# Two counting steps and three fine steps in the searches for experts 3 to 6

## The chip, the cores and the metric

The kernel runs on one core of a Trainium2 chip. The metric is the device time of one execution in microseconds (us), from profiles and timings on the chip. The engines named here are TensorE (PE in the profile, PEld for its weight loads), VectorE (DVE), ScalarE (ACT), GpSimd (POOL) and SyncE (SP), whose queue issues most DMAs.

## The reference

An attention with a decaying state makes 3072 rows of 384. A mixture of eight experts assigns each row to one expert, greedily by falling logit, with at most 384 rows per expert; each expert is a two-layer network. A second network with squared ReLU follows on all rows.

```python
logits = x @ w_gate
order = np.argsort(-logits.flatten())
for idx in order:
    tok, e = (int(idx) // E, int(idx) % E)
    if assigned[tok] >= 0 or counts[e] >= cap:
        continue
    assigned[tok] = e
    counts[e] += 1
for e in range(E):
    mask = assigned == e
    h = np.maximum(x[mask] @ w1[e], 0.0)
    out[mask] = h @ w2[e]
h = np.maximum(out @ w_in, 0.0)
return h * h @ w_out
```

## The kernel before

After the attention (its last part is over at about 105 us of the span) the kernel finds the experts one after another: the expert that fills first, its 384 rows, then the next among the rows and experts that are left. "Expert p" is the p-th one found, p = 0 to 7. The work on expert p, `expert(p)` and then `mlp(p)`, is a dense row of large matmuls of 384 columns; every product is made of three matmuls, from high and low parts (XH and XL, wh and wl, ah and al, YH and YL). ScalarE makes the high parts, VectorE or GpSimd the low ones.

The search for expert p+1 runs beside the work on expert p. `tick()` stands after each block of nine large matmuls, 47 times per expert (16 in `expert`, 31 in `mlp`), and there advances the generator `phase(p+1)` by one `yield`. Matmuls of the search are thus sown among the large ones in the order in which the program issues them; the order on TensorE and SP is this written order, and on VectorE, ScalarE and GpSimd it is made by the scheduler of the framework.

One step of a search (L697 to L773) tests 64 thresholds. VectorE compares 3072 keys (128 partitions x 24) with all of them in three operations (L537, called at L705); TensorE counts by expert in twelve small matmuls (L715), folds two halves with two more (L756) and sums the saturated ones with a matmul against ones (L765); VectorE takes the maximum (L769) and the new lower bound (L772). Four such steps give a bracket [lo, hi) for the threshold at which the expert fills. The selection follows (L782 on): it counts the sure and the possible rows (L793, L794), scans them, makes two staircases E0 and E1 over 384 slots (L814, L816), and turns them into row numbers by six matmuls (L823, L824); GpSimd gathers the rows (L840).

For p of 2 and more the gathered rows are transposed in blocks: SP writes them to a scratch in DRAM (`xb`) and reads them back in another order into two tiles of a ring of five (`raw64`), and VectorE transposes 32x32 blocks into PSUM (L867, alternately `misc` and `conv`), from which XH and XL are made. The copy at L866 holds each transpose behind the newest al. As soon as an expert is known, SP loads its weights (five raw tiles), which ScalarE and GpSimd split into wh (L926) and wl (L927).

The search for p+1 begins with the first tick of expert p. It needs 21 ticks to the selection and 41 to the last block.

Of the kernel before, what the change touches and what calls it, by code (L numbers as in the profile page):

```python
# [40 lines left out]
E = 8  # L41
# [3 lines left out]
BLOCKS = 2  # L45
# [415 lines left out]
class Routing:  # L461
# [4 lines left out]
    def __init__(self, tc, pool, ident, L):  # L466
# [5 lines left out]
        self.lag = 3, 1  # L472
# [187 lines left out]

    def phase(self, p, st, xd, rows, half):
# [6 lines left out]
        sc = w([128, 24], "scal")  # L668
        rs = w([128, 2], "rs", BF)
        scn = w([128, 2, NT], "scn")  # L670
        if last:
            for _ in range(18):
                yield
# [4 lines left out]
        else:  # L678
            if p:
                sh = [128, NT, E]  # L680
                lm = w(sh, "lm", FT, 1)
                if p == 2:
                    V.tensor_copy(lm[0:1, 0, 0:1], self.made())
                V.tensor_tensor(lm, self.L, pen[:, None, :].to_broadcast(sh), op=OP.add)
                m, key, cx, oh = w([128, NT], "m"), w([128, NT], "key"), w([128, NT], "cx"), w(sh, "oh", BF)
                V.tensor_reduce(m, lm, axis=AX.X, op=OP.max)
                V.tensor_tensor(key, m, dead, op=OP.add)
                for f in self.pick(lm, m, cx, oh, w(sh, "eq", FT, 1)):
                    f()
                yield  # L690

                base, d = self.low[:, 0:1], self.range
            else:
                key, cx, oh = self.key0, self.cx0, self.oh0
                base, d = self.s0[:, 0:1], self.s0[:, 1:2]
            steps = range(0 if p else 1, 4)
            for t in steps:  # L697
                fin = t == steps[-1]
                cnt = self.misc()
                thr = cnt[:, 256:256 + KG] if p else w([128, KG], "thr")  # L700
                V.tensor_scalar(thr, self.k[:, 1:], d, base, op0=OP.mult, op1=OP.add)
                cuts = (0, 8, 16, 24) if p else (0, 9, 18, 24)
                cms = []

                def cmp():  # L705
                    a, b = cuts[len(cms)], cuts[len(cms) + 1]
                    cms.append(w([128, b - a, KG], "cm", BF, 3))
                    self.compare(V, cms[-1], key[:, a:b], thr)

                def cmm(g):  # L710
                    for j in range(cuts[g], cuts[g + 1], 2 if p else 1):
                        i = j - cuts[g]
                        if p:

                            PE.matmul(cnt[:, :2 * E], cms[g][:, i:i + 2].rearrange("p j k -> p (j k)"),  # L715
# [599 lines left out]
```

## Time and profile before

| | before |
|---|---|
| median of 3 runs (lowest, highest) | 783.78 us (783.5, 786.86) |
| profiled execution: time | 782.99 us |
| its span, first to last instruction | 781.3 us |
| TensorE busy, matmuls | 757.0 us (97%) |
| VectorE busy | 432.2 us (55%) |
| ScalarE busy | 383.6 us (49%) |
| GpSimd busy | 300.3 us (38%) |
| mean granted TensorE clock, share of full speed | 0.983 |

"Busy" is the union of an engine's instructions over the span. Matmuls overlap in the pipeline, so that a busy TensorE is no proof that it works at its peak; distances from one start to the next are the better measure. An idle time is put down to the instruction that ended it. In a timeline the columns are start (us), duration (us), engine, line, operation, output and inputs, shapes and count; a count above one merges a row of equal instructions.

### The profile page before, as it was taken

The numbers are of one execution on the slowest core, as the hardware profiler recorded it, in microseconds if no ns is written. First come the engines' busy times: TensorE is split into PE (matmuls) and PEld (weight loads), VectorE is DVE, ScalarE is ACT, GpSimd is POOL, SyncE is SP. The second block draws the span as 40 slices with busy tenths as digits, with TensorE's granted clock in tenths as the row PEclk, the third lists the DMA queues.
The fourth block names the chain that finished last, engine by engine and source line by source line (L and its number), as shares of the span: only waits on it lengthen the run. The fifth ranks groups of instructions, "written<-read, shape, count | busy, mean of one in ns | idle before, by whom it ended". The sixth has DMA issues, their size and how long they took to land.

```text
span 781.3 us, 16728 instructions
## 1 busy us (share of the span) xinstructions
PE 757.0 (97%) x6388; PEld 713.1 (91%) x6389; DVE 432.2 (55%) x1118; ACT 383.6 (49%) x886; POOL 300.3 (38%) x321
## 2 busy tenths in 40 slices
PE   7999996899999999999999999999999999999996
PEld 4888874698999999999999999999999999999996
DVE  9899998988964554455445444534453423221210
ACT  3666651546662465346534643464346455452542
POOL 6899831667653061306130614060406072013001
PEclk9999995999999999999999999999999999999999
DMA  9988751674351071107010701070107040400000
GB/s 257 281 249 258 224 185 54 209 227 124 102 188 31 8 206 39 33 4 215 27 40 1 223 20 42 0 210 35 41 1 208 33 135 11 133 25 27 1 0 31
DMA packets 48689, 80.84 MB, mean 103 GB/s; under 512 B 14448, under 2 KB 36448, under 8 KB 48608
## 3 DMA queue, kind: packets, MB, share of 16 engines
q1 hardware_dynamic: 45536, 70.33, 30.3%
q0 software_dynamic: 3072, 9.44, 3.6%
q8 instruction: 50, 0.82, 0.5%
q14 instruction: 31, 0.25, 0.1%
HBM read 66.78 MB, written 12.98 MB: 102 GB/s over the span
## 4 chain that ended last, share of the span: by engine, by line
PE 86%; DVE 8%; DMA 2%; issue 2%; POOL 1%; ACT 1%; SPq 0%; POOLq 0%; DVEq 0%; ACTq 0%
PE acc L930 12%; PE ph L930 12%; PE acc L932 12%; PE acc L931 12%; PE ph L931 12%; PE ph L932 12%; PE pA L247 3%; PE pY L267 3%; DMA raw<-in_w_dram 2%; PE ph L1056 1%; PE pl L284 1%; PE pt L304 1%; PE pk L327 1%; PE pY L260 1%; PE misc L715 1%
## 5 line engine op out<-in xcount | busy, mean ns | idle before, releaser
L927 POOL TENSOR_TENSOR wl<-raw,wh 128x384 fp32r<-128x384 f32 x114 | 115.0, 1027 | 184.8 <-ACT wh L926 153.1
L1114 DVE TENSOR_TENSOR al<-ph,ah 128x384 fp32r<-128x384 f32 x105 | 58.4, 556 | 135.1 <-ACT ph L1106 134.8
L930 PE MATMUL ph<-YH,wi 128*128 128x384 f32 x384 | 132.1, 344 | 0.0
L931 PE MATMUL ph<-YL,wi 128*128 128x384 f32 x384 | 129.3, 337 | 1.2 <-DVE YL L1085 1.2
L930 PE MATMUL acc<-wo,ah 128*128 128x384 f32 x384 | 129.5, 337 | 0.0
L932 PE MATMUL acc<-wo,al 128*128 128x384 f32 x384 | 128.8, 335 | 0.7 <-POOL al L1114 0.7
L932 PE MATMUL ph<-YH,wi 128*128 128x384 f32 x384 | 128.9, 336 | 0.0
L931 PE MATMUL acc<-wo,ah 128*128 128x384 f32 x384 | 128.5, 335 | 0.0
L1099 ACT ACTIVATE t<-ph 128x384 f32<-128x384 f32 x128 | 62.1, 492 | 111.5 <-PE ph L932 100.3
L1132 POOL DMA_INDIRECT out_dram<-rows,idx x24 | 23.7, 988 | 205.0 <-ACT rows L1130 200.8
L926 ACT ACTIVATE wh<-raw 128x384 fp32r<-128x384 f32 x128 | 66.0, 523 | 74.2 <-DMA raw<-in_w_dram 24.6
L1066 DVE SCALAR_TENSOR_TENSOR al<-ph,ah 128x384 fp32r<-128x384 f32 x64 | 35.6, 556 | 82.8 <-ACT ah L1063 82.8
L931 PEld LDWEIGHTS ph<-YL,wi 128*128 128x128 f32 x384 | 72.2, 188 | 2.2 <-DVE YL L1085 2.0
L932 PEld LDWEIGHTS acc<-wo,al 128*128 128x128 f32 x384 | 72.1, 188 | 1.4 <-POOL al L1114 1.0
L930 PEld LDWEIGHTS ph<-YH,wi 128*128 128x128 f32 x384 | 72.2, 188 | 0.0
L930 PEld LDWEIGHTS acc<-wo,ah 128*128 128x128 f32 x384 | 72.1, 188 | 0.0
L931 PEld LDWEIGHTS acc<-wo,ah 128*128 128x128 f32 x384 | 72.1, 188 | 0.0
L932 PEld LDWEIGHTS ph<-YH,wi 128*128 128x128 f32 x384 | 72.1, 188 | 0.0
L1105 ACT ACTIVATE ah<-t 128x384 fp32r<-128x384 f32 x128 | 67.2, 526 | 2.7
L930 PE MATMUL acc<-ah,wh 128*128 128x384 f32 x192 | 66.3, 345 | 0.1
L932 PE MATMUL acc<-ah,wl 128*128 128x384 f32 x192 | 64.5, 336 | 0.6 <-POOL wl L927 0.6
L931 PE MATMUL acc<-al,wh 128*128 128x384 f32 x192 | 64.3, 335 | 0.0
(263 smaller groups left out, 1516.5 us busy)
## 6 DMA issues: line engine op xcount, KB each, us to landing
raw<-in_w_dram SPq DMA_DIRECT2D x128, 192.0 KB, 2.9
rk<-in_rk_dram SPq DMA_DIRECT2D x24, 448.0 KB, 5.3
tk<-in_tk_dram SPq DMA_DIRECT2D x24, 392.0 KB, 5.8
raw<-in_wi_dram SPq DMA_DIRECT2D x16, 384.0 KB, 3.6
raw<-in_wo_dram SPq DMA_DIRECT2D x16, 384.0 KB, 3.5
xd<-xs SPq DMA_DIRECT2D x24, 192.0 KB, 3.1
xb<-rows SPq DMA_DIRECT2D x18, 192.0 KB, 3.1
raw<-xb SPq DMA_DIRECT2D x18, 192.0 KB, 3.9
```

Of the source, the lines that this page charges most:

```text
L247: PE.matmul(pA[n][s][half(c, 64), i], RK[n][half(s), 1, i, 64 * c:64 * c + 64], RK[n][half(s), 0, i], start=True, stop=True)
L267: PE.matmul(pYs[n][s][half(i % 2, 64), i // 2], v_of(n, 2 * i + s), AM[n][:, i, s], start=not c and i < 2, stop=True, skip_group_check=True)
L926: A_.activation(hi, t, AF.Copy)
L927: (eng or G).tensor_tensor(lo, t, hi.bitcast(FT), op=OP.subtract)
L930: PE.matmul(o, l[0], r[0], start=first, stop=False)
L931: PE.matmul(o, l[0], r[1], start=False, stop=False)
L932: PE.matmul(o, l[1], r[0], start=False, stop=last)
L1066: V.scalar_tensor_tensor(hl, o, 0.0, hh.bitcast(FT), op0=OP.max, op1=OP.subtract)
L1099: A_.activation(t, o, AF.Relu)
L1105: A_.activation(gh, t, AF.Square)
L1114: (V if p else G).tensor_tensor(gl, t2, gh.bitcast(FT), op=OP.subtract)
L1132: h = G.indirect_dma_start(out=out, out_offset=bass.IndirectOffsetOnAxis(ap=st[p]["idx"][:, i:i + 1], axis=0), in_=t, in_offset=None)
```

## The change

For experts 3 to 6 a search has five steps. The first two are the counting steps of before, the second with a sixteenth as the next spacing. The three that follow test 16 thresholds by VectorE alone: the partition stands for one of 16 thresholds and one of 8 experts, and four operations compare 768 keys each and add up the result. For that the keys, masked by expert (`lay`, two operations), go to a scratch in DRAM (`kd`) in one DMA and come back in four, each to all 16 thresholds, in tiles of the ring `raw64`. A fine step has one matmul: the saturated flags, one column repeated as 128 columns of weights, against a constant `its`. That matmul stands five ticks (`gap`) after the step; the first fine step also waits six ticks. GpSimd and VectorE make the constants once, beside expert 1.

The searches are one stream: the search for an expert begins when the rows of the one ahead of it are gathered, not with the first tick of an expert. The selection of experts 3 to 6 is held back to tick 17 of the expert that runs. The block transposes become a task of their own beside the stream; they take one ring tile and one fixed tile, use `conv` alone in PSUM, and have seven ticks instead of four between the read and the transposes. The last phase waits 38 ticks instead of 18, from its earlier start.

In all selections E0 less E1 is made first (one operation of VectorE with two inputs instead of a comparison and a negation), and three matmuls make the slots instead of six.

```diff
-BLOCKS = 2
+BLOCKS, KS, HUNT, WIDE = 2, 16, 3, 2
...
-        self.lag = 3, 1
+        self.lag, self.gap = (3, 1), 5
+        self.tasks = []
...
+    def lay(self, key, cx):
+
+        V, w = self.tc.nc.vector, self.tile
+        km = w([128, E, NT], "eq", FT, 1)
+        bc = lambda t: t[:, None, :].to_broadcast([128, E, NT])
+        V.tensor_tensor(km, self.rev[:, :, None].to_broadcast([128, E, NT]), bc(cx), op=OP.not_equal)
+        V.scalar_tensor_tensor(km, km, -BIG, bc(key), op0=OP.mult, op1=OP.add)
+        return km
...
+    def blocked(self, st, xg, half):
+
+        nc = self.tc.nc
+        V, A_ = nc.vector, nc.scalar
+        for _ in range(5):
+            yield
+        for i in range(3):
+            nc.sync.dma_start(self.xb[i].rearrange("a p c -> p a c"), xg[i].rearrange("p (a c) -> p a c", a=4))
+        for _ in range(3):
+            yield
+        t = self.wide_row()
+        zs = t[:, :384], t[:, 384:], self.tile([128, 384], "zs", FT, 1)
+        for i in range(3):
+            nc.sync.dma_start(zs[i], self.xb[i].rearrange("a (i b) c -> (a i) (b c)", b=4))
+        for _ in range(7):
+            yield
+        st['x'] = XH, XL = half("XH"), half("XL")
+        for i in range(3):
+            px = self.spare()[:, :CAP]
+            V.tensor_copy(px[0:1, 0:1], self.latest())
+            V.transpose(px, zs[i].rearrange("p (b c k) -> p b k c", b=4, k=3))
+            by = lambda t: t[:, :, 128 * i:128 * i + 128].rearrange("p k (t b) -> p k b t", b=4)
+            pxv = px.rearrange("p (b k t) -> p k b t", b=4, k=3)
+            A_.activation(by(XH), pxv, AF.Copy)
+            V.tensor_tensor(by(XL), pxv, by(XH).bitcast(FT), op=OP.subtract)
+            yield
+        st['ready'] = True
...
-            for _ in range(18):
+            for _ in range(38):
...
+                fine = p >= HUNT
+                oh = w([128, NT, E], "oh", BF)
+                key, cx = self.choose(p, oh)
+                kE, todo = [], []
+                if fine:
+                    km = self.lay(key, cx)
+
+                    def out():
+                        nc.sync.dma_start(self.kd.rearrange("e (p j) -> p e j", j=NT), km)
+
+                    def back():
+                        for g in range(4):
+                            kE.append(self.wide_row())
+                            nc.sync.dma_start(kE[g], self.kd[None, :, 768 * g:768 * g + 768].to_broadcast([KS, E, 768]))
+
+                    todo = [None, out, None, None, back] + [self.grid_sums] * (p == HUNT)
+
+                def go():
+                    f = todo.pop(0) if todo else None
+                    if f:
+                        f()
...
-            steps = range(0 if p else 1, 4)
+            steps = range(5) if p >= HUNT else range(0 if p else 1, 4)
             for t in steps:
                 fin = t == steps[-1]
...
+                fine = p >= HUNT and t >= WIDE
+                per = KS if p >= HUNT and t + 1 >= WIDE else KG
+                if fine:
+                    if t == WIDE:
+                        for _ in range(6):
+                            yield
+                    thr, part = w([128, 1], "thr1"), w([128, 5], "part")
+                    V.tensor_scalar(thr, self.kp, d, base, op0=OP.mult, op1=OP.add)
+                    for g in range(4):
+                        hit = w([128, NT * 32], "hit", BF, 1)
+                        V.tensor_scalar(hit, kE[g], thr, 0.0, op0=OP.is_ge, op1=OP.add, accum_out=part[:, g:g + 1])
+                    V.tensor_scalar(part[:, 4:5], part[:, 0:1], part[:, 1:2], part[:, 2:3], op0=OP.add, op1=OP.add)
+                    sat = w([128, 1], "sat1", BF)
+                    V.tensor_scalar(sat, part[:, 4:5], part[:, 3:4], CAP - 0.5, op0=OP.add, op1=OP.is_ge)
...
+                    for _ in range(self.gap):
+                        yield
...
+                if fine:
+                    PE.matmul(ne[:, :E], sat.to_broadcast([128, 128]), self.its, start=True, stop=True)
+                else:
+                    PE.matmul(ne[:, :E], self.ones if p else self.ones[:KG, :], sat, start=True, stop=True)
...
+        while p >= HUNT and not last and self.soon():
+            yield
...
-        V.tensor_scalar(E0, self.slot, o[:, 0:1], None, op0=OP.is_ge)
+        V.tensor_scalar(E1, self.slot, o[:, 1:2], None, op0=OP.is_ge)
         V.scalar_tensor_tensor(dat[:, 1:NT + 1], scn[:, 1], pp[:, 1:2], scn[:, 0], op0=OP.add, op1=OP.min)
-        V.tensor_scalar(E1, self.slot, o[:, 1:2], None, op0=OP.is_ge)
-        neg = w([128, NT + 1], "neg", HF)
-        V.tensor_scalar(neg, dat[:, 1:], -1.0, None, op0=OP.mult)
+        V.scalar_tensor_tensor(E0, self.slot, o[:, 0:1], E1, op0=OP.is_ge, op1=OP.subtract)
         yield
         pc = self.misc()
         pcv = pc[:, :96].rearrange("p (i c) -> p i c", i=3)
         for i in range(3):
-            PE.matmul(pcv[:, i, :NT + 1], E0[:, 128 * i:128 * i + 128], dat[:, 1:], start=True, stop=False)
-            PE.matmul(pcv[:, i, :NT + 1], E1[:, 128 * i:128 * i + 128], neg, start=False, stop=True)
+            PE.matmul(pcv[:, i, :NT + 1], E0[:, 128 * i:128 * i + 128], dat[:, 1:], start=True, stop=True)
...
+        if p >= BLOCKS:
+            self.tasks.append(self.blocked(st, xg, half))
+            if p == HUNT - 1:
+                self.grid()
+            yield 'gather'
+            return
...
-    bg, rate = [iter(())], [0.0]
+    rate, begun = [0.0], [0]
+
+    def stream():
+        for p in range(1, E):
+            yield from R.phase(p, st[p], xd, row, half)
+
+    search = stream()
+
+    def proceed():
+        next(search, None)
+        if R.tasks and next(R.tasks[0], R) is R:
+            R.tasks.pop(0)
...
-                next(bg[0], None)
+                proceed()
...
+    R.soon = lambda: now[0] - begun[-1] < 17
...
-        bg[0] = route(p + 1) if p + 1 < E else iter(())
...
-        for _ in bg[0]:
-            pass
+        while p + 1 < E and not st[p + 1].get('ready'):
+            proceed()
...
```

## Rows read from the trace of the kernel before

**Rows 1.** Stretches: length; busy PE, PEld, DVE, ACT, POOL; clock, DMA share, GB/s.
```profile
230.81:623.21 392.40, 392.40 (x2507) 380.70 (x2506) 191.04 (x538) 187.99 (x406) 109.97 (x111) 1.00 0.24 71
623.21:698.93 75.72, 75.72 (x443) 75.13 (x442) 21.85 (x48) 37.92 (x82) 21.93 (x23) 1.00 0.25 74
```

**Rows 2.** Timeline of TensorE around the counting and ones matmuls of one step, expert 3.
```profile
395.39 0.34 PE L932 MATMUL ph<-XH,wl 128*128 128x384 f32 x1
395.57 0.46 PE L715 MATMUL misc<-oh,cm 128*128 128x16 bf16 x12
...
396.14 0.34 PE L931 MATMUL acc<-al,wh 128*128 128x384 f32 x1
...
399.14 0.34 PE L932 MATMUL ph<-XH,wl 128*128 128x384 f32 x1
399.31 0.18 PE L765 MATMUL misc<-sat,onesb 128*128 128x8 bf16 x1
...
399.62 0.34 PE L931 MATMUL acc<-al,wh 128*128 128x384 f32 x1
```

**Rows 3.** Timeline of TensorE at the first matmuls on YL, experts 5 and 6.
```profile
571.98 0.40 PE L931 MATMUL ph<-YL,wi 128*128 128x384 f32 x1
572.21 0.34 PE L932 MATMUL ph<-YH,wi 128*128 128x384 f32 x1
...
648.17 0.34 PE L930 MATMUL ph<-YH,wi 128*128 128x384 f32 x1
648.46 0.45 PE L931 MATMUL ph<-YL,wi 128*128 128x384 f32 x1
648.75 0.34 PE L932 MATMUL ph<-YH,wi 128*128 128x384 f32 x1
```

**Rows 4.** Timeline of TensorE around the slot matmuls of one selection, expert 3.
```profile
433.06 0.34 PE L932 MATMUL acc<-wo,al 128*128 128x384 f32 x1
433.23 0.19 PE L823 MATMUL misc<-dat,E 128*128 128x25 f16 x1
...
433.66 0.34 PE L931 MATMUL ph<-YL,wi 128*128 128x384 f32 x1
```

**Rows 5.** Timeline of VectorE after that ones matmul, into the next step.
```profile
399.55 0.17 DVE L769 TENSOR_REDUCE n<-misc 128x1 f32<-128x8 f32 x1 [1.58 <-PE misc L765]
399.75 0.27 DVE L772 TENSOR_SCALAR scal<-n,scal,low 128x1 f32<-128x1 f32 x1
400.06 0.35 DVE L701 TENSOR_SCALAR misc<-k,scal 128x64 f32<-128x64 f32 x1
400.31 0.55 DVE L1066 SCALAR_TENSOR_TENSOR al<-ph,ah 128x384 fp32r<-128x384 f32 x1
400.78 1.87 DVE L537 TENSOR_TENSOR cm<-key,misc 128x512 bf16<-128x512 f32 x3
```

**Rows 6.** Groups of VectorE by form: busy us, mean ns of one, idle before.
```profile
L552 DVE TENSOR_SCALAR_CACHE_REDUCE sel<-low 128x24 f32<-128x24 f32 x2 | 0.4, 178 | 0.0
L537 DVE TENSOR_TENSOR cm<-key,thr 128x384 bf16<-128x384 f32 x3 | 1.6, 550 | 0.0
...
L537 DVE TENSOR_TENSOR cm<-key,misc 128x512 bf16<-128x512 f32 x58 | 37.1, 681 | 0.1
L814 DVE TENSOR_SCALAR E<-slot,o 128x384 f16<-128x384 f16 x6 | 1.9, 312 | 0.0
```

**Rows 7.** DMA issues by line: KB each, median us from issue to landing.
```profile
raw<-in_wi_dram SPq DMA_DIRECT2D x16, 384.0 KB, 3.6
raw<-xb SPq DMA_DIRECT2D x18, 192.0 KB, 3.9
```

**Rows 8.** Timeline of GpSimd, then VectorE with GpSimd busy and idle.
```profile
353.28 3.34 POOL L927 TENSOR_TENSOR wl<-raw,wh 128x384 fp32r<-128x384 f32 x3 [30.79 <-ACT wh L926]
...
353.40 1.02 DVE L818 TENSOR_SCALAR neg<-dat 128x25 f16<-128x25 f16 x1
...
431.91 0.17 DVE L818 TENSOR_SCALAR neg<-dat 128x25 f16<-128x25 f16 x1
```

More of the change, by code (lines that the diff above doesn't have):

```diff
@@ new lines, in grid_sums, with choose @@
+    def grid_sums(self):
+        V = self.tc.nc.vector
+        one = lambda shape, name, dt=FT: self.pool.tile(shape, dt, name=name, bufs=1)
+        t, i, r = (self.raster[:, j] for j in range(3))
+        self.its, self.kp = one([128, E], "its", BF), one([128, 1], "kp")
+        V.tensor_reduce(r[:, 0], t.rearrange("p t e -> p e t"), axis=AX.X, op=OP.add)
+        V.tensor_copy(self.its, r[:, 0])
+        V.scalar_tensor_tensor(t, i, 1.0, t, op0=OP.mult, op1=OP.mult, accum_out=self.kp)
+    def choose(self, p, oh):
+        V, w = self.tc.nc.vector, self.tile
+        sh = [128, NT, E]
+        lm = w(sh, "lm", FT, 1)
+        if p == 2:
+            V.tensor_copy(lm[0:1, 0, 0:1], self.made())
+        V.tensor_tensor(lm, self.L, self.pen[:, None, :].to_broadcast(sh), op=OP.add)
+        m, key, cx = w([128, NT], "m"), w([128, NT], "key"), w([128, NT], "cx")
+        V.tensor_reduce(m, lm, axis=AX.X, op=OP.max)
+        V.tensor_tensor(key, m, self.dead, op=OP.add)
+        ops = self.pick(lm, m, cx, oh, w(sh, "eq", FT, 1))
+        for f in ops if oh is not None else ops[:3]:
+            f()
+        return key, cx
@@ L679, in phase @@
             if p:
[L680 to L689, printed above, removed]
+                fine = p >= HUNT
[14 more added lines that the diff above has]
+                    if f:
+                        f()
                 yield
@@ L695, in phase @@
                 base, d = self.s0[:, 0:1], self.s0[:, 1:2]
-            steps = range(0 if p else 1, 4)
+            steps = range(5) if p >= HUNT else range(0 if p else 1, 4)
             for t in steps:
                 fin = t == steps[-1]
[L699 to L715, printed above, removed]
-                                      oh[:, j:j + 2].rearrange("p j e -> p (j e)"), start=j == 0, stop=j == NT - 2)
-                        else:
-                            PE.matmul(cnt[:KG, :E], cms[g][:, i], oh[:, j], start=j == 0, stop=j == NT - 1)
-                cmp()
-                if not p:
@@ L748, in phase @@
                     self.fill(t > 1)
-                if p:
+                if fine:
+                    pass
+                elif p:
                     own = w([128, 2, E], "own", HF)
@@ L760, in phase @@
                         yield
+                        go()
                 else:
@@ L764, in phase @@
                 ne = self.misc()
-                PE.matmul(ne[:, :E], self.ones if p else self.ones[:KG, :], sat, start=True, stop=True)
+                if fine:
+                    PE.matmul(ne[:, :E], sat.to_broadcast([128, 128]), self.its, start=True, stop=True)
+                else:
+                    PE.matmul(ne[:, :E], self.ones if p else self.ones[:KG, :], sat, start=True, stop=True)
                 if not p:
@@ L1137, in expert @@
     def expert(p):
+        begun.append(now[0])
         for f in range(FB1):
@@ L1201, in blocks @@
         return t[0][:, :384], t[0][:, 384:], t[1][:, :384]
-    R.blocks = blocks
     R.made = lambda: st[1]["x"][1][0:1, 2, CAP - 1:CAP].bitcast(FT)
```

71 lines of the change are left out of this document (42 added, 29 removed).

## The prediction

> **What bounds the kernel now.** I read the page's first two parts first (in the table above): TensorE is busy for 97% of the span and its granted clock is at its upper level in all 40 slices but one. So time can only go where TensorE's own queue gets shorter or longer. The busy times by expert say this more sharply [rows 1]: from the start of expert 1 to the start of expert 6 TensorE is busy for all 392.40 us, five experts of 78.48 us. In each of these a search of four steps runs for the next expert. Expert 6 has none beside it (expert 7 takes what is left) and lasts 75.72 us, with the same large matmuls. A search therefore costs 2.76 us of TensorE, and VectorE, busy for half of the time, costs nothing as long as nobody waits for it. That difference is the budget out of which the change can pay.
>
> Then the timeline of TensorE shows what one step costs [rows 2]. Large matmuls start 0.174 us apart. Between the one at 395.39 and the one at 396.14 lie the twelve small counting matmuls and one large: 0.75 us where two distances would be 0.35, so 0.40 for the twelve. The one matmul with the ones matrix stretches two distances to 0.48 (399.14 to 399.62): 0.13 to 0.14. The remaining piece, two folding matmuls, is what is left of the step.
>
> One correction: in expert 6 the first matmuls on YL wait for VectorE; the starts 648.17, 648.46 and 648.75 are 0.12 and 0.12 longer than a distance, 0.23 in all. In expert 5, where a fold stands just ahead of that place, the wait that is left is 0.23 less 0.17, 0.06 [rows 3]. A search thus hides 0.17 us of another wait, and four steps cost 2.76 + 0.17 = 2.93 us, 0.73 a step.
>
> **The change part by part.** *Two steps fewer in the counting form, for experts 3 to 6.* 8 steps of 0.73: 5.84 us less.
>
> *Three fine steps with one matmul each.* Its shape is that of the ones matmul (128 columns of weights in bf16, 8 moving), so 0.14: 12 x 0.14 = 1.68 us more. Its weights are one column repeated, which no row shows; the fold's place bounds it above (0.73 - 0.40 - 0.14 = 0.19), so 1.7 to 2.3 us. I take 1.7, as shape and type are those of the ones matmul.
>
> *Slots by one difference.* Six matmuls become three per selection. The six stretch two distances from 0.35 to 0.60 (433.06 to 433.66) [rows 4]: 0.25, of which the first costs 0.14 as the ones matmul does and five more about 0.025 each. Three fewer are 0.08; seven selections lie under dense TensorE: 0.55 us less. The first selection, ahead of expert 0, loses an operation on VectorE but gets a longer one; I count 0, with 0.1 either way.
>
> *The wait for YL.* The search of expert p now has its last fine matmul some ten ticks into expert p-1 and selects from tick 17, just after YL. No counting step stands at YL any more, so each of experts 1 to 5 should show the wait of expert 6.
>
> *The sum.* Experts 1 to 5 are built from expert 6: 5 x 75.72 = 378.60, less 5 x 0.08 for slots, plus 12 counting steps (four for expert 2, two for each of 3 to 6) x 0.73 = 8.76, plus 1.68: 388.64, against 392.40: 3.8 us less. Slots in experts 0 and 6 give 0.16 more. So **3.9 us less** by TensorE alone. On the profiled execution (span 781.3, 783.0 in all) that is 779.1; I set it against the median, 783.8, which lies 0.8 above that execution: **779.9 us**, 0.5% less.
>
> *What VectorE must do for it.* This holds only if the new waits are met. TensorE is in order, so the fine matmul, which waits for *sat* of its step, holds all large matmuls behind it. It is placed five ticks after the step's start, 45 large matmuls of 0.174: 7.82 us. In that time VectorE runs: n (0.2 to the next start), the new bound (0.3) [rows 5], the threshold (0.3), four comparisons of 768 keys with a sum, and two small sums (0.3 each). A comparison that also sums exists in the trace with 24 elements: 0.178. Its price for 768 is bounded by two rows [rows 6]: one element per 1.02 ns, from 512 against 384 elements of the counting comparison (681 and 550 ns), gives 0.178 + 744 x 1.02 ns = 0.94. The plain comparison of slots does 384 elements of f16 in 0.31, 0.14 more than 25 elements take (0.17) [rows 6, 8]: at that rate 768 take 0.46. I take 0.94, the sum being the nearer row in kind; the spacing is some 0.08 less, as three counting comparisons of 0.68 take 1.87 [rows 5], and the scalar read from memory may add as much. So the chain is 0.25 (matmul to n) + 0.2 + 0.3 + 0.3 + 4 x 0.92 + 0.6 = 5.3 us, some 5.5 with the reading of the sums. Two or three evictions of al share the window at 0.5 each [rows 5]: 6.5 to 7.0. That leaves 0.8 to 1.3 us; the other end, 0.46 each, leaves 2.7 and more. The step that follows the two counting steps has six ticks more ahead of it and shares VectorE with the three block transposes, which now pass one after the other through a single PSUM buffer; but its threshold is known before them, so its comparisons may fill the gaps in which they wait for ScalarE.
>
> *Who waits behind the comparisons on VectorE.* al of an expert's hidden block is needed four block passes (6.3 us) after its matmuls. ScalarE's eviction ahead of it and its own, 0.55 [rows 5], leave room for some 4 us behind four comparisons before TensorE notices. Nothing is added there.
>
> *DMAs.* SP now also issues a write of the keys, which waits for VectorE, and three ticks later four reads of 384 KB. Behind them stand the weights of the next expert (needed some 16 ticks later) and the three block reads, one tick behind. A 384 KB read of today's lands in 3.6 us, most of it latency, a block read in 3.9 [rows 7]; four large ones at the same rate with no overlap would take 14.4 us, with the overlap that a queue gives some 8. The block reads have seven ticks, 11 us, now (four before): hidden in the second case, about 3 to 6 us late in the first, of which al can absorb some 4. I count 0. With the cover gone TensorE would lose up to 2 us per expert, 8 in all.
>
> **A rule that speaks against it.** A small plain operation of VectorE that needs 0.17 when GpSimd is idle took 1.02 us beside GpSimd's weight subtractions (353.40, inside the 3.34 us from 353.28) [rows 8]. So some forms of VectorE wait for GpSimd. The Trainium skill, "SBUF — State Buffer" (SBUF: two separate sides), says that the two share a port pair that whoever starts first holds for its whole instruction; "VectorE: DVE Perf Modes" (The perf-mode tier table) says that an fp32 tensor_scalar from SBUF runs in such a two-port mode at twice the rate. By that rule the comparisons would be faster alone and would collide with GpSimd in the expert's first ten microseconds. No row shows a summing form in that mode; the next part prices it as a mechanism of its own.
>
> **Rivals.** (a) *The comparisons collide with GpSimd.* Place: the last two fine steps, which run while GpSimd makes the first weights of an expert. Each comparison then waits for a subtraction (3.34 us for three, 1.1) and runs 0.46 to 0.7, between its bounds: about 1.65 each, 6.6 instead of 3.7, chain 8.4, with al 9.4 to 9.9, so 1.6 to 2.1 us too late; 8 such steps, 13 to 17 us. From 1.15 to 1.25 us per comparison on, TensorE waits. Time: 779.9 + 15 = **795**, slower. For it: one plain comparison with a single SBUF input did wait. Against it: no summing form is seen to. 0.13.
> (b) *VectorE's order.* The window is enough, but al, block transposes and comparisons are interleaved badly and 0.3 us is lost in each of 12 fine steps: 3.6 us back, **783.5**, no change. For it: the margin of 0.8 to 1.3 us is small beside a single idle wait of VectorE, 1.58 us, for a matmul [rows 5]. 0.25.
> (c) *The reads of keys delay the blocks*, up to 8 us: about **786**. Against it: an expert uses 71 GB/s on average [rows 1], and 1.6 MB more in 78 us are 20. 0.05.
> (d) *Less than it says*: the repeated-column weights cost 0.19 or more: **780.5**. 0.1.
>
> **How the numbers follow.** Forecast, no new wait: 0.47, 779.9 with 0.6 either way. A measurement of this kernel can tell 0.5%, 3.9 us, so "faster" begins at 779.9, in the middle of the forecast: 0.24 of it is faster, and I add 0.16 for counting steps whose removal brings more than their matmuls (the large matmuls after them also start 0.18 apart for a while). Faster 0.40; same 0.43 (the rest of the forecast, b, d, half of c); slower 0.17. Range: 778.6 to 785.5, which takes in b and d and leaves a out.
>
> **What would show it.** Right: experts 1 to 5 last about 77.7 us each instead of 78.48; per search two groups of twelve counting matmuls and three lone ones; summing comparisons near 0.95 to 1.0 us, whether GpSimd works or not; no gap of TensorE ahead of the fine matmuls. Wrong: idle weight loads ahead of the fine matmul put down to *sat* (a, b); comparisons of uneven length while GpSimd is busy (a); transposes idle before them put down to a DMA (c); a fine matmul that stretches the distance by over 0.19 (d).

## The result and the profile after

The changed kernel is slower, by 0.3 to 0.6%. Beside the kernel before it took 789.62 us (median of 15 runs, 786.05 to 793.39) against 784.65 us (15 runs, 782.72 to 786.86): a ratio of 1.0061, 95% interval 1.0044 to 1.0077. In a second session it came to 1.0034 (1.0014 to 1.0055). The forecast was 779.9 us and its range ended at 785.5.

The profiled execution took 789.53 us, with a span of 787.5 us against 781.3. The first view is by stretches, one for each of experts 0 to 6; columns as in [rows 1], which they answer.

```profile
147.40:236.99 89.59, 83.97 (x507) 80.11 (x508) 74.20 (x179) 50.76 (x110) 54.90 (x56) 0.96 0.53 164
236.99:319.35 82.36, 80.52 (x531) 76.71 (x530) 52.81 (x139) 37.62 (x82) 22.85 (x26) 1.00 0.33 88
319.35:398.75 79.40, 77.95 (x473) 75.64 (x473) 49.10 (x142) 37.86 (x82) 21.57 (x23) 1.00 0.33 91
398.75:476.28 77.53, 77.53 (x472) 75.52 (x472) 46.82 (x134) 38.06 (x82) 21.71 (x23) 1.00 0.34 94
476.28:553.83 77.55, 77.55 (x473) 75.54 (x473) 46.80 (x134) 38.08 (x82) 21.73 (x23) 1.00 0.33 94
553.83:629.70 75.87, 75.87 (x441) 74.96 (x441) 31.94 (x91) 37.92 (x82) 21.70 (x23) 1.00 0.25 73
629.70:705.14 75.44, 75.44 (x439) 75.09 (x439) 22.25 (x47) 38.07 (x82) 22.11 (x23) 1.00 0.26 74
```

Compare each with what the prediction's terms give. With 75.64 us for an expert without a search, 0.73 for a counting step and 0.14 for a fine one, expert 1 (six counting steps, one fine matmul at its end) is 80.16, experts 2 to 4 (two and three) 77.52 and expert 5 (two fine) 75.92.

| | expert 0 | 1 | 2 | 3 | 4 | 5 |
|---|---|---|---|---|---|---|
| before | 85.33 | 78.51 | 78.44 | 78.51 | 78.44 | 78.49 |
| from the forecast's terms | 85.25 | 80.16 | 77.52 | 77.52 | 77.52 | 75.92 |
| after | 89.59 | 82.36 | 79.40 | 77.53 | 77.55 | 75.87 |

Experts 3 to 5 are right to 0.05 us. What is missing lies in three places: 2.2 us in expert 1, 1.9 in expert 2, and 4.3 in expert 0 with 1.9 more ahead of it. In experts 1 and 2 TensorE is busy for 1.84 and 1.45 us less than the stretch is long; in [rows 1] it was busy for the whole of it. The waits of TensorE from expert 1 to the end of expert 2 say for whom (total, times, longest; the page's source lines are those of the changed kernel, where L862 is the fold, L933 the slot matmuls, L1024 to L1026 the large matmuls):

```profile
PE misc L862 <- DVE own L856: 1.6, 1, 1.6
PE ph L1024 <- ACT YH L1189: 1.3, 1, 1.3
PE misc L933 <- DVE dat L935: 0.3, 1, 0.3
PE ph L1025 <- DVE YL L1190: 0.2, 1, 0.2
```

None of them is a wait for *sat*. The fine steps themselves are as forecast. VectorE in one step (timeline), and TensorE around the next fine matmul:

```profile
395.72 0.17 DVE L879 TENSOR_REDUCE n<-misc 128x1 f32<-128x8 f32 x1 [1.12 <-PE misc L873]
...
396.55 1.01 DVE L793 TENSOR_SCALAR_CACHE_REDUCE hit<-raw,thr 128x768 bf16<-128x768 f32 x1
397.48 0.08 DVE L793 DVE_READ_ACCUMULATOR hit<-raw,thr 128x1 f32 x1
397.60 1.01 DVE L793 TENSOR_SCALAR_CACHE_REDUCE hit<-raw,thr 128x768 bf16<-128x768 f32 x1
...
400.95 0.22 DVE L796 TENSOR_SCALAR sat<-part 128x1 bf16<-128x1 f32 x1
```

```profile
403.26 0.34 PE L1026 MATMUL ph<-XH,wl 128*128 128x384 f32 x1
403.44 0.18 PE L873 MATMUL misc<-its,sat 128*128 128x8 bf16 x1
403.48 0.42 PE L1024 MATMUL acc<-ah,wh 128*128 128x384 f32 x1
403.74 0.34 PE L1025 MATMUL acc<-al,wh 128*128 128x384 f32 x1
```

From n to the end of *sat* are 5.45 us (395.72 to 401.17), the fine matmul comes 2.3 us later, and it stretches two distances to 0.48 (403.26 to 403.74), as [rows 2] had it for the ones matmul. The summing comparisons of all twelve fine steps, as one group (shortest, median and longest in ns):

```profile
L793 DVE TENSOR_SCALAR_CACHE_REDUCE hit<-raw,thr x48: 1001/1012/1015, 303.2 to 563.2; 128x768 bf16<-128x768 f32 x48
```

Of these 48, 13 began while GpSimd subtracted weights; they took as long as the others.

The first trace of before shows one execution, and a short one, as a second trace shows below: there expert 0 began 1.6 us later and took 1.9 us longer. So the two waits of experts 1 and 2 were taken up first.

### The profile page after: what moved, and what is told of

Its sections match the earlier page's. It is cut to its first block, busy times and chain, and to the rows that moved or that the text cites. A ratio compares the mean times of both kernels' runs of the same rounds, so it can differ in the third digit from the quotient of the medians.

```text
span 787.5 us, 16600 instructions
## 1 busy us (share of the span) xinstructions
PE 756.7 (96%) x6257; PEld 713.0 (91%) x6257; DVE 472.3 (60%) x1218; ACT 385.1 (49%) x886; POOL 300.7 (38%) x325
## 4 chain that ended last, share of the span: by engine, by line
PE 83%; DVE 10%; DMA 2%; issue 2%; ACT 1%; POOL 1%; SPq 0%; POOLq 0%; DVEq 0%; ACTq 0%
PE acc L1024 12%; PE ph L1024 12%; PE ph L1025 11%; PE acc L1026 11%; PE acc L1025 11%; PE ph L1026 11%; PE pA L247 3%; PE pY L267 3%; DMA raw<-in_w_dram 2%; PE pt L304 1%; PE ph L1161 1%; PE pl L284 1%; PE pk L327 1%; PE pY L260 1%; DVE cm L538 1%
## 5 line engine op out<-in xcount | busy, mean ns | idle before, releaser
L1024 PE MATMUL ph<-YH,wi 128*128 128x384 f32 x384 | 131.7, 343 | 1.3 <-ACT YH L1189 1.3
L1024 PE MATMUL acc<-wo,ah 128*128 128x384 f32 x384 | 132.1, 344 | 0.0
L1026 PE MATMUL acc<-wo,al 128*128 128x384 f32 x384 | 129.3, 337 | 0.7 <-POOL al L1219 0.7
L1026 PE MATMUL ph<-YH,wi 128*128 128x384 f32 x384 | 129.7, 338 | 0.0
L1025 PE MATMUL acc<-wo,ah 128*128 128x384 f32 x384 | 129.2, 337 | 0.0
L1171 DVE SCALAR_TENSOR_TENSOR al<-ph,ah 128x384 fp32r<-128x384 f32 x64 | 35.5, 555 | 70.3 <-ACT ah L1168 70.1
L1024 PEld LDWEIGHTS ph<-YH,wi 128*128 128x128 f32 x384 | 72.6, 189 | 1.6 <-ACT YH L1189 1.6
L1026 PEld LDWEIGHTS acc<-wo,al 128*128 128x128 f32 x384 | 72.6, 189 | 1.0 <-POOL al L1219 1.0
L1024 PEld LDWEIGHTS acc<-wo,ah 128*128 128x128 f32 x384 | 72.7, 189 | 0.0
L1026 PEld LDWEIGHTS ph<-YH,wi 128*128 128x128 f32 x384 | 72.6, 189 | 0.0
L1024 PE MATMUL acc<-ah,wh 128*128 128x384 f32 x192 | 65.1, 339 | 0.0
L1026 PE MATMUL acc<-ah,wl 128*128 128x384 f32 x192 | 64.3, 335 | 0.5 <-POOL wl L1021 0.5
```

Of the source, the lines that this page charges most:

```text
L1024: PE.matmul(o, l[0], r[0], start=first, stop=False)
L1025: PE.matmul(o, l[0], r[1], start=False, stop=False)
L1026: PE.matmul(o, l[1], r[0], start=False, stop=last)
L1171: V.scalar_tensor_tensor(hl, o, 0.0, hh.bitcast(FT), op0=OP.max, op1=OP.subtract)
```

## The experiments

The lengths that the traces gave (us; "start" is that of expert 0), each kernel beside the kernel before in the same session. For the kernel before the ratio is that of the control.

| kernel | start | expert 0 | 1 | 2 | 3 | ratio to before (95%) |
|---|---|---|---|---|---|---|
| before | 145.48 | 85.33 | 78.51 | 78.44 | 78.51 | |
| before, again | 147.11 | 87.19 | 78.49 | 78.45 | 78.49 | 1.0013 (0.9995 to 1.0031) |
| changed | 147.40 | 89.59 | 82.36 | 79.40 | 77.53 | 1.0061 (1.0044 to 1.0077) |
| changed, again | 146.51 | 89.80 | 82.39 | 80.99 | 77.53 | 1.0034 (1.0014 to 1.0055) |
| cast on ScalarE | 150.79 | 88.03 | 82.32 | 81.31 | 77.53 | 1.0052 (1.0030 to 1.0074) |
| selection behind YL | 146.74 | 89.43 | 82.42 | 86.24 | 85.77 | 1.0445 (1.0409 to 1.0482) |
| slots as before | 148.61 | 87.54 | 84.32 | 78.96 | 77.60 | 1.0024 (1.0003 to 1.0045) |
| sums later | 152.12 | 87.67 | 80.69 | 79.27 | 77.53 | 1.0014 (0.9995 to 1.0032) |
| loads behind YL | 146.57 | 85.96 | 82.38 | 86.54 | 85.95 | 1.0439 (1.0417 to 1.0461) |
| sums, loads, old slots | 150.24 | 85.84 | 80.56 | 86.98 | 86.15 | 1.0406 (1.0376 to 1.0436) |
| before with new slots | 148.23 | 86.37 | 78.45 | 78.40 | 78.45 | 1.0038 (1.0019 to 1.0058) |
| four ticks | 147.01 | 88.53 | 82.48 | 77.70 | 77.53 | 1.0012 (0.9992 to 1.0032) |
| four ticks, sums later | 145.67 | 85.85 | 80.78 | 77.71 | 77.53 | 0.9989 (0.9971 to 1.0007) |
| the same, old slots first | 145.73 | 85.17 | 80.62 | 77.71 | 77.53 | 0.9980 (0.9962 to 0.9997) |

### The changed kernel again

> The changed kernel unaltered, beside the kernel before. Theory A (fixed waits): the 5 us lost come from waits with a place, so they stand in this trace again: about 1.5 us at the first fold of expert 1 (behind VectorE's 3.65 us cast of the counts of thresholds), about 1.4 us at the first G matmul behind expert 2 (ScalarE's YH behind weight splits), and 2.4 us instead of 1.5 at the transposes of expert 1's rows; the ratio comes to 1.006. Theory B (chance): the waits were those of one execution; here they are gone or stand elsewhere, and the difference to before lies in stretches at the lower granted clock and in the attention ahead of the experts. Theory A splits the loss of 1.9 us ahead of expert 0 and some 3 us of lower clock in expert 0 off as open: this trace says whether either comes back.

Both waits stand where they stood, at 1.6 (fold) and 1.4 us (YH); the transposes waited 1.91. Expert 1 is within 0.04 us of the first trace. They have a place; the start of expert 0 and the 1.6 us between the two lengths of expert 2 do not.

### Expert 1: who holds *own*

*own* holds the counts that the two fold matmuls of a counting step read. In the changed kernel, VectorE ahead of *own*, and GpSimd beside it:

```profile
286.05 0.40 DVE L677 TENSOR_REDUCE hit<-hit 128x8 f32<-128x128 f32 x1
286.38 0.54 DVE L1219 TENSOR_TENSOR al<-ph,ah 128x384 fp32r<-128x384 f32 x1
286.84 3.65 DVE L678 CAST its<-hit 128x8 bf16<-128x8 f32 x1
290.41 0.28 DVE L679 SCALAR_TENSOR_TENSOR hit<-hit 128x128 f32<-128x128 f32 x1
...
291.53 0.16 DVE L856 TENSOR_TENSOR own<-misc,mine 128x16 f16<-128x16 f32 x1
```

```profile
286.55 3.90 POOL L1021 TENSOR_TENSOR wl<-raw,wh 128x384 fp32r<-128x384 f32 x4
```

A cast of eight numbers lasts 3.65 us and ends with GpSimd's four subtractions (286.55 + 3.90 = 290.45). It belongs to the three sums over the grid of 16 thresholds and 8 experts, from which the constants of the fine steps come. They are made once, in the second counting step of expert 3's search, which runs beside expert 1. First only the cast was moved:

```diff
-        V.tensor_copy(self.its, r[:, 0])
+        self.tc.nc.scalar.activation(self.its, r[:, 0], AF.Copy)
```

> The changed kernel with one instruction moved: the cast of the eight counts of thresholds to bf16 from VectorE to ScalarE. Theory A: the 3.65 us that the cast took beside GpSimd's four subtractions of weights go, own comes about 3 us earlier, the 1.56 us wait of the first fold in expert 1 falls under 0.3, and the kernel is 1.3 to 1.6 us faster than the changed one run beside it (ratio to before near 1.004). A rival: any VectorE instruction that stands there waits just as long (GpSimd holds what they share), so own is as late as it was and nothing is gained. Theory B: no change beyond chance.

The wait stayed, at 1.49 us, as the rival had it. VectorE's next instruction of the three took the cast's place; with GpSimd's row:

```profile
288.65 3.79 DVE L679 SCALAR_TENSOR_TENSOR hit<-hit 128x128 f32<-128x128 f32 x1
...
293.29 0.17 DVE L856 TENSOR_TENSOR own<-misc,mine 128x16 f16<-128x16 f32 x1
```

```profile
288.38 3.90 POOL L1021 TENSOR_TENSOR wl<-raw,wh 128x384 fp32r<-128x384 f32 x4
```

An instruction that needs 0.28 us at 290.41 needs 3.79 here. So it is not the cast but the place. Then all three sums were moved:

```diff
-                    todo = [None, out, None, None, back] + [self.grid_sums] * (p == HUNT)
+                    todo = [None, out, None, None, back] + [None, None, None, None, self.grid_sums] * (p == HUNT)
...
+        V.tensor_copy(r[0:1, 0, 0:1], self.latest())
         V.tensor_reduce(r[:, 0], t.rearrange("p t e -> p e t"), axis=AX.X, op=OP.add)
         V.tensor_copy(self.its, r[:, 0])
-        V.scalar_tensor_tensor(t, i, 1.0, t, op0=OP.mult, op1=OP.mult, accum_out=self.kp)
+        V.scalar_tensor_tensor(r, i, 1.0, t, op0=OP.mult, op1=OP.mult, accum_out=self.kp)
```

> The changed kernel with the three sums over the grid (counts of thresholds, their cast, their number by key) moved as a whole: they wait for a later al and come behind the first own of expert 3's second counting step. Taking only the cast off VectorE had let the instruction behind it last 3.79 us beside GpSimd's four subtractions. Theory A2 (VectorE's instruction with SBUF operands waits out GpSimd's burst, and own stands behind it): with none of the three ahead of own, the wait of the first fold in expert 1 falls from 1.5 to under 0.3 us, expert 1 takes about 80.8 instead of 82.4 us, and the ratio comes to 1.001 to 1.002. The rival: the next instruction with SBUF operands (dn, bn, b2, or the al) takes the wait over, and own is as late as before; expert 1 stays at 82.4. Theory B: the difference is one of clock and chance and the ratio stays at 1.003 to 1.006.

The waits of TensorE in experts 1 and 2 of this kernel, in which every line number is one higher:

```profile
PE ph L1025 <- ACT YH L1190: 1.2, 1, 1.2
PE misc L934 <- DVE dat L936: 0.3, 1, 0.3
```

The fold's wait is gone, expert 1 is 1.7 us shorter, and the ratio is 1.0014. The cast, now at 300.8, lasts 0.17 us. None of the instructions that stood behind the sums took the wait over, as the rival would have it. So the two runs show that the sums ahead of *own* made this wait. That it is GpSimd's burst that they wait for is read from the rows: in both kernels the long instruction ends with the burst to 0.2 us.

The Trainium skill, "SBUF — State Buffer" (SBUF: two separate sides), says that VectorE and GpSimd share a port pair as an exclusive lock, for VectorE's two-port modes, which a tensor_scalar that also writes out its sum does not enter, and for its instructions with two SBUF inputs. These rows agree for the 128x128 sum with two SBUF inputs (3.79 against 0.28 us) and, if the cast ran in such a mode, which no run here shows, for the cast (3.65 against 0.17). The summing comparisons agree too, at 1.00 to 1.015 us beside GpSimd or not, and so does al, one of whose inputs is in PSUM: 38 of the hidden block's al (L1171) began in the changed kernel while GpSimd subtracted, and took 0.55 to 0.56.

### Expert 2: who holds YH

In the changed kernel, ScalarE ahead of YH:

```profile
344.08 0.53 ACT L1020 ACTIVATE wh<-raw 128x384 fp32r<-128x384 f32 x1 [0.68 <-DMA raw<-in_w_dram]
345.17 0.52 ACT L1020 ACTIVATE wh<-raw 128x384 fp32r<-128x384 f32 x1 [0.56 <-DMA raw<-in_w_dram]
345.60 0.47 ACT L1189 ACTIVATE YH<-acc 128x384 fp32r<-128x384 f32 x1
346.31 0.52 ACT L1020 ACTIVATE wh<-raw 128x384 fp32r<-128x384 f32 x1 [0.24 <-DMA raw<-in_w_dram]
```

Splits of expert 3's weights, each waiting for a load, stand ahead of YH in ScalarE's order. The loads start when the index of expert 3 (*ei*, which SP reads) is known:

```profile
L904 DVE TENSOR_SCALAR ei<-scal x1: 148/148/148, 336.3 to 336.3; 128x1 int32<-128x1 f32 x1
```

That is 17.0 us into expert 2; for the later indices it is 13.8 us into experts 3 to 5. YH starts at 26.3 us in expert 2 and at 24.4 in the others. In the kernel before the index came 40.1 us into each, long behind YH. Two edits tried to make it late again. The first held the selection:

```diff
+            if p >= HUNT:
+                V.tensor_copy(ei[0:1, 0:1], self.split_y(p - 1))
             V.tensor_scalar(ei, rv, -1.0, float(E), op0=OP.mult, op1=OP.add)
```

(*split_y* is the last element of YL of the expert that is running.)

> The changed kernel with the selection of experts 3 to 6 made to wait for data: a one element copy of the last YL into ei's place stands ahead of ei, so the index of the expert, and with it the loads and splits of its weights, comes behind YL rather than 9 us ahead of it. Theory A: the 1.30 and 0.15 us waits for YH and YL behind expert 2 go, and what YL waits there are in experts 3 to 5 (0.23 us each) fall too: 1.4 to 2.0 us faster than the changed kernel beside it. The rival: ScalarE is late at YH for its own queue of activations, not for the weights, and the wait stays at over 1 us; or the later weights are late for the next expert's first matmuls, which shows as new waits for wh or wl of 1 us or more, and takes back the gain.

This cost 7 to 8 us in each of experts 2 to 5. Neither theory had it: TensorE waits for VectorE's al, 6.0 us in each of experts 2 to 4 and 5.0 in expert 5. The second held only the loads:

```diff
+        if HUNT <= p < E - 1 and n == 0:
+            V.tensor_copy(raws[i][0:1, 0:1], st[p - 1]["y"][1][0:1, 2, CAP - 1:CAP].bitcast(FT))
         nc.sync.dma_start(raws[i], src[bass.ds(st[p]["e"], 1), n % FB1].rearrange("a p m -> (a p) m"))
```

> The changed kernel with the selection left as early as it runs, but the loads of weights of experts 3 to 6 behind the last YL of the expert before (one element of YL is copied into the first weight's buffer ahead of its load). Holding the selection itself had cost 8 us an expert, since its line on VectorE stood ahead of al. Theory A: ScalarE's YH no longer stands behind splits that wait for these loads; the 1.30 and 0.15 us behind expert 2 go, and the stretch at the lower clock behind them (1.5 us in two of three traces) with them. Expert 2 takes 77.6 to 78 us instead of 79.4 to 81.3, and the kernel is 1.5 to 3 us faster than the changed one, ratio 0.9995 to 1.002. The rival: the loads, now 9 us later, are late for expert 3's first matmuls or hold the reads of keys behind them on SP's queue: new waits of over 1 us at fine steps or at the first H matmuls, ratio 1.004 or more.

It cost the same, by its rival's ratio but not at its place, and its rows say where. The waits of TensorE in expert 2, then VectorE and GpSimd:

```profile
PE ph L1024 <- DVE al L1221: 3.5, 1, 3.5
PE acc L1026 <- DVE al L1221: 1.4, 1, 1.4
```

```profile
349.23 1.07 DVE L926 TENSOR_SCALAR E<-slot,o 128x384 f16<-128x384 f16 x1
350.21 0.99 DVE L927 SCALAR_TENSOR_TENSOR dat<-scn,misc 128x24 f16<-128x24 f32 x1
351.12 1.41 DVE L928 SCALAR_TENSOR_TENSOR E<-slot,o,E 128x384 f16<-128x384 f16 x1
...
353.45 0.92 DVE L954 SCALAR_TENSOR_TENSOR dead<-sel,dead 128x24 f32<-128x24 f32 x1
...
354.51 0.55 DVE L1221 TENSOR_TENSOR al<-ph,ah 128x384 fp32r<-128x384 f32 x1
```

```profile
348.85 5.49 POOL L1021 TENSOR_TENSOR wl<-raw,wh 128x384 fp32r<-128x384 f32 x5
```

The late loads bring GpSimd's subtractions just when VectorE makes the slots. The four instructions take 1.07, 0.99, 1.41 and 0.92 us; in the changed kernel, with GpSimd idle, the same four take 0.31, 0.24, 0.61 and 0.17. al stands behind them, and TensorE behind al. Behind these waits the granted clock stands at 0.50 from 350.2 to 360.0, which is most of the rest of the 8.8 us that this expert 2 is longer than the cured one below. YH does come in time here (339.90, 25.0 us into the expert); the gain is paid back several times over. With these loads, the later sums and the old slots together:

> The changed kernel with the sums later, the loads behind YL, and the slots as before. Theory A: expert 1 about 81 us (with the old slots' matmuls), expert 2 about 78, experts 3 to 6 as in the changed kernel (77.6, 77.6, 75.9, 75.5), expert 0 at 86 to 88 by the stretches of lower clock: 781 to 784 us, ratio 0.996 to 1.000. Theory B (the loss is the clock and chance): 786 to 788 us, ratio 1.002 to 1.005.

Expert 1 was cured (80.56), experts 2 to 5 were not. So the loads must come earlier, not later. The next edit brings expert 3's three fine steps a tick nearer to each other:

```diff
-                    for _ in range(self.gap):
+                    for _ in range(self.gap - (p == HUNT)):
```

> The changed kernel with the fine steps of expert 3's search four ticks apart instead of five (the other searches as they are). In the traces the index of expert 3 is known 17.0 us into expert 2, those of experts 4 to 6 13.8 us into their experts, and only expert 2 has YH late, at 26.4 instead of 24.4 us. Theory A: three steps a tick (about 1.5 us) nearer bring the index to 12.5 to 14 us, the weights land before YH is due, YH starts at 24.4 and the 1.3 and 0.15 us waits go, with the stretch at the lower clock where there was one: expert 2 takes 77.5 to 78.0 us, and the ratio is 0.002 to 0.004 under that of the changed kernel (1.0034 and 1.0061). The rival: the chain of 5.6 us doesn't fit into four ticks, TensorE waits 0.3 us or more for sat in each of the three steps, and expert 2 is no shorter than 79 us.

*ei* comes 12.8 us into expert 2, which begins at 318.02, and ScalarE no longer meets a late load ahead of YH (*ei*, then the timeline's two rows at YH):

```profile
L904 DVE TENSOR_SCALAR ei<-scal x1: 152/152/152, 330.8 to 330.8; 128x1 int32<-128x1 f32 x1
...
341.92 0.52 ACT L1020 ACTIVATE wh<-raw 128x384 fp32r<-128x384 f32 x1 [1.04 <-PE acc L1025]
342.56 1.01 ACT L1189 ACTIVATE YH<-acc 128x384 fp32r<-128x384 f32 x2
```

YH starts at 24.5 us, the wait is gone, expert 2 takes 77.70. That is 0.17 more than expert 3: the second fine matmul stretches its two distances to 0.64 instead of 0.48, so four ticks are just enough for the chain.

### The slots

The slots went back to the old form in the changed kernel (two comparisons, *neg*, six matmuls), and the new form alone went into the kernel before:

```diff
+        V.tensor_scalar(E0, self.slot, o[:, 0:1], None, op0=OP.is_ge)
...
-        V.scalar_tensor_tensor(E0, self.slot, o[:, 0:1], E1, op0=OP.is_ge, op1=OP.subtract)
+        neg = w([128, NT + 1], "neg", HF)
+        V.tensor_scalar(neg, dat[:, 1:], -1.0, None, op0=OP.mult)
...
```

> The changed kernel with the slots as before: two comparisons, the negated list and six matmuls, in all eight selections. Theory A: the selection chain of expert 1 is again about 1 us shorter, so the transposes of its rows wait 1.5 us rather than 2.4, and the selection of expert 0 gives back 0.2 us; the three more matmuls cost about 0.5 us over the seven selections beside TensorE's work (8 times 0.08). Net 0.3 to 0.6 us faster than the changed kernel, and up to 1.6 us more if the lower clock behind the transposes comes of that longer wait. The rival: the chain of expert 1 is late because of what GpSimd does beside it and not of the new operation; the wait stays at 2.4 us and the kernel is 0.5 us slower.

> The kernel before with the change's slots alone: one difference of two comparisons and three matmuls. Theory A: the three matmuls less give back 0.08 us in each of seven selections, 0.55 us, but VectorE's difference lasts 0.60 us where a comparison and the negation lasted 0.31 and 0.17; where the chain is on the path (experts 0 and 1) its chain ends 0.4 to 1.0 us later and TensorE waits 0.3 to 0.4 us for it: 783.5 to 785 us, ratio 0.999 to 1.001. The rival: the slots alone account for most of expert 0's 2 to 4 us: ratio 1.003 to 1.005. Expert 0's length against 85.33 us tells.

(Expert 1's 84.32 us in the first of the two has a wait of 2.1 us for the fold and a stretch at the lower clock behind it.) Where nothing waits the new form gains what was forecast: expert 3 takes 77.60 us with the old slots and 77.53 with the new. In expert 0 the chain is on the path. TensorE at the slot matmuls of the changed kernel:

```profile
214.37 0.24 PE L933 MATMUL misc<-dat,E 128*128 128x25 f16 x3 [0.41 <-DVE E L928]
```

The wait is 0.40 to 0.41 in all nine traces with the new form here, 0.12 in the five with the old. As the new form has three matmuls less, the distance of the large matmuls on either side grows by less, from 0.66 to 0.68 us to 0.83 to 0.84. The difference takes 0.61 us on VectorE where a second comparison and *neg* took 0.31 and 0.17 [rows 6, 8]. Over all traces expert 0 takes 87.9 us on average with the new form (85.9 to 89.8) and 86.2 with the old (85.2 to 87.5). The ranges overlap. Alone, the new slots came to 0.38% (0.19 to 0.58), 3.0 us, which is the rival's ratio and more than these waits. But in that run's trace 2.75 of the 3.45 us that it is longer than the first trace of before lie ahead of expert 0, where the slots stand only at the first selection (0.2 us). The kernel before itself, run again, came to 0.13% with an interval that overlaps this one. So only the 0.2 us at the first selection and the longer wait in expert 0 are shown.

### The kernel before again

> The kernel before, unaltered, for a second trace of it and for the spread of its runs. The first trace began expert 0 at 145.48 us and had expert 0 at 85.33 us; the nine traces of changed kernels began it at 146.5 to 152.1 us, with the difference arising at 12 to 44 us, in the attention. Theory C (chance): this trace too begins expert 0 anywhere from 145 to 152 us, has waits of 1.5 to 2.4 us at the transposes of expert 1's rows and now and then a stretch at the lower clock behind them; ratio 1.000 within 0.002. The rival (the changes lengthen these): again near 145.5 and 85.3 us, and the changed kernels' front and expert 0 owe 2 to 4 us to what was changed.

Expert 0 began 1.6 us later than in the first trace and took 1.9 us longer, from the same program. Its transposes waited 1.85 us, and behind them the clock fell. The stretch behind the transposes here and in the changed kernel; the third number from the right is the granted clock:

```profile
228.20:231.20 3.00, 3.00 (x11) 3.00 (x11) 2.70 (x6) 1.14 (x3) 1.01 (x1) 0.53 0.51 138
```

```profile
230.90:234.40 3.50, 3.50 (x15) 3.50 (x15) 3.13 (x8) 1.14 (x3) 1.01 (x1) 0.62 0.47 144
```

Large matmuls start 0.32 us apart there instead of 0.174: the lower of the two levels, 1.2 GHz. Ten or eleven matmuls of that cost 1.5 us. Eight of fourteen traces have it, after waits of 1.77 to 2.37 us; six have not, after 1.50 to 2.20. So it comes with the longer waits at the transposes, but not with each. The kernel before has it too, in one of two traces, so it needs no part of the change; two traces are too few to say whether the change makes it more frequent.

The 4.3 us of expert 0 between the first two traces can now be split. TensorE is idle there for 5.62 us instead of 4.28, and its matmuls are busy 2.9 us longer: that is the stretch behind the transposes and a second one of ten matmuls at the lower clock, behind the wait for YL. The ten microseconds around that wait, before and after:

```profile
170.00:180.00 10.00, 8.83 (x62) 8.11 (x61) 9.57 (x23) 4.91 (x11) 4.14 (x5) 1.00 0.68 187
172.00:182.00 10.00, 8.40 (x46) 7.64 (x43) 8.04 (x19) 3.35 (x8) 3.57 (x4) 0.83 0.61 186
```

This second stretch stands in three of the fourteen traces (the changed kernel's two, and the selection behind YL), all of changed kernels; what decides it is not shown.

### Both cures, and the slots of experts 0 to 2

The sums later and four ticks together; then, in addition, the old slots for experts 0 to 2 and the new ones from 3 on (an *if p < HUNT* around the lines above).

> The changed kernel with both: the sums over the grid behind the first own, and expert 3's fine steps four ticks apart. Theory A: expert 1 at 80.7 us, expert 2 at 77.5 to 78.0, the rest as in the changed kernel, so 1.5 to 3 us less than the run with the sums alone (1.0014): ratio 0.997 to 1.000. The rival: the ratio stays at 1.001 or more, since the loss lies ahead of expert 1.

> As the run before, and with the slots of experts 0 to 2 as before the change (two comparisons, the negated list, six matmuls), those of experts 3 to 7 by one difference. The slots alone, set into the kernel before, cost 0.4%, more than the waits in their one trace explain (0.4 us at the slot matmuls, 0.2 us at the first selection, 0.7 us at the transposes). Theory A: 0.3 us at the wait for the slot matmuls in expert 0 and 0.28 us in expert 1 go, 0.2 us at the first selection, up to 0.8 us at the transposes, against 0.2 us for nine more matmuls: 0.5 to 1.5 us faster than the run before, ratio 0.996 to 0.999. The rival: the slots cost nothing that the runs can tell from chance, and the two runs are equal within 0.002.

The first of them, experts 1 and 2 (columns as in [rows 1]):

```profile
231.53:312.31 80.78, 80.50 (x531) 76.76 (x531) 52.98 (x148) 37.66 (x82) 22.85 (x26) 1.00 0.33 90
312.31:390.01 77.70, 77.70 (x472) 75.53 (x472) 47.92 (x138) 37.81 (x82) 21.83 (x23) 1.00 0.34 93
```

Its experts 1 to 5 take 389.44 us (231.53 to 620.97), 3.0 less than before; the forecast said 388.64. It ran in 784.02 us (780.53 to 785.95), level with before: its trace is of its fastest execution, and no trace shows where the others lose what experts 1 to 5 gained. With the old slots ahead it ran in 783.67 us (780.09 to 784.96) against 784.09 (35 runs): 0.998, 0.9962 to 0.9997, the only kernel here whose interval lies below 1, and only just. The two are equal within 0.002, as the rival had it, though the waits that were to go in experts 0 and 1 went.

## Why the prediction was wrong

**The terms of TensorE were right.** Counting steps, fine matmuls, slots under dense work and the wait for YL give experts 3, 4 and 5 to 0.05 us, and with both waits cured the sum over experts 1 to 5 to 0.8. Of that 0.28 is the wait for the slot matmuls in expert 1 and 0.17 the tighter fine steps in expert 2; the rest, some 0.3 in expert 1, is not explained.

**"Selects from tick 17, just after YL" was wrong.** Ticks order what is issued, and here VectorE ran ahead of them: it made *ei* 13.8 to 17.0 us into the expert, right behind the last fine matmul, where tick 17 is at some 28 us (an estimate, 17/47 of 77.5). SP loaded the weights at once. I had counted the loads as needed 16 ticks later and asked nothing of the splits, which ScalarE does ahead of YH. The cost was 1.45 us of waits in expert 2 (1.7 us of its length against the cured kernel), with 1.5 more in the traces in which the clock fell behind that wait. The cure by the opposite sign shows it: 4.2 us earlier, no wait.

**"Nothing is added there" was wrong.** It was asked of the comparisons only. The three sums over the grid, which run once, were in the change and not in the sum. Undisturbed they last 0.40, 0.17 and 0.28 us; they cost TensorE 1.56 and, with them moved, expert 1 is 1.7 us shorter. They fell on a burst of GpSimd, and *own* stood behind them. The row that warned of it, 1.02 us for a 0.17 us instruction beside GpSimd [rows 8], was weighed for the comparisons, where it doesn't hold, and for nothing else.

**The first selections: "0, with 0.1 either way".** The first selection ends some 0.2 us later, and the slot matmuls beside expert 0 wait 0.3 us more and cost 0.16 more, where 0.08 less was forecast. No wait was asked for in expert 0, and the selection that runs beside it is one that TensorE waits for.

**The rivals.** (a) fell: all 48 summing comparisons lasted 1.00 to 1.015 us, beside GpSimd or not, so the rule that spoke against the change does not reach this form. (b) fell: no fine matmul waited for *sat* with five ticks, and 2.3 us were left in the step shown. (c) fell: no wait for a block or a key; the four reads of a search had landed 9.6 to 10.8 us after the first was issued, between the 8 and the 14.4 of the prediction. (d) fell: a fine matmul costs 0.13. The wait in expert 2 came from a rival that I did not write: that what is begun early arrives in someone else's queue.

**The base.** The sum was set against one execution and the median of three, which agreed. The second trace of before differs from the first by 3.5 us up to the end of expert 0, 1.6 of it ahead of expert 0. Of the 6.2 us by which expert 1 begins later in the changed kernel's first trace than in the first of before, a part of that size can thus be chance. The slots are shown to cause 0.4 us of it (0.2 at the first selection, 0.16 at the slot matmuls); how much more they caused remains open. With both waits cured the kernel is only level with before and not 3.9 us faster, so the forecast time would have been missed without the two waits as well, and the cause of that part is open.

## What to carry to other kernels

For each step that a change makes possible earlier, ask which engine will run it as soon as its data is there, and what then stands behind it on the other engines: here the index was known 23 to 26 us sooner, the loads began at once, and their splits took YH's place in ScalarE's order. Price instructions that run only once like all others, by their place: three small sums cost 1.6 us of TensorE where they stood, and nothing some 11 us later. Before a loss of a few us is explained, take a second trace of the kernel before.

## What the runs showed of the hardware

A summing comparison of VectorE (128x768, f32 from SBUF, bf16 out) takes 1.01 us and does not wait for GpSimd (13 of 48 began beside it), with 0.08 more to read the sum; they follow each other every 1.05 us. Some other instructions of VectorE do wait for GpSimd, in two ways: the cast and the sum with two SBUF inputs waited through all four subtractions of a burst (3.65 and 3.79 us), while the four instructions of a selection took some 0.75 us more each, less than one subtraction (5.49 us for five). What decides between the two was not tried. A matmul whose weights are one column repeated 128 times stretches two distances of the large matmuls to 0.48 us, as one with a plain matrix of ones does.
